# Leaving out three junk matmuls in the run-up of a fused recurrence and gated-MLP kernel

## The chip, the cores and the metric

The kernel runs on one core of a Trainium2 chip. The metric is the device time of one execution in microseconds; before the change it is 146.53 us, the median of three runs (146.23 to 146.56). The profiled execution has a span of 144.7 us from the first to the last instruction, and all times below count from the start of that span.

The engines are named as in the profile: PE is TensorE (PEld its weight loads), DVE VectorE, ACT ScalarE, POOL GpSimd, and SP the engine that issues the DMA transfers.

## The reference

Two stages follow each other. The first is a gated linear recurrence over 768 positions for 4 batches of 8 heads of 48 columns; the second an MLP with a spatial gate on the result. Cut to what matters:

```python
# q, k, v, alpha: (4, 8, 768, 48) fp32
for t in range(S):
    state = alpha[:, :, t, :, None] * state + einsum('bhd,bhe->bhde', k[:, :, t], v[:, :, t])
    y[:, :, t] = einsum('bhd,bhde->bhe', q[:, :, t], state)
x = y.transpose(0, 2, 1, 3).reshape(4, 768, 384)

h = maximum(x @ w_in, 0)                     # w_in: 384 x 1024
u, v = h[..., :512], h[..., 512:]
v_n = (v - mean(v)) / sqrt(var(v) + 1e-6)
v_s = einsum('ts,bsd->btd', w_spatial, v_n) + b_spatial[None, :, None]
out = (u * v_s) @ w_out                      # (4, 768, 384) fp32
```

## The kernel before

The recurrence is computed in chunks of 128 positions, six for each batch, 24 in all. Within a chunk the products over time are matrix products: PE sums log(alpha) with a triangular matrix (`cum`), ACT takes exponentials of the sums with both signs (`binv`, and the bank itself), k is multiplied with the one and q with the other (`kt`, `qt`, on DVE or POOL), PE transposes both (L481), ACT or DVE copies the transposes out of PSUM (`kqT`), PE forms the scores (L553), DVE masks them (`ptm`, L564), and PE multiplies the masked scores with v (L580) and q with the state so far (L593). The state goes from chunk to chunk through PE (L523), DVE (L330 and L332), POOL (L337) and a bf16 copy by POOL (`sbd`, L199). The first eight chunks are taken two at a time, in pairs, whose halves are the even and odd positions; pair 0 and pair 1 are the run-up that the change touches. The MLP of a batch follows its chunks and is interleaved with the chunks of later batches.

All PSUM tiles come from one ring of eight banks: the function `bank` hands them out in turn, so that each PE operation that needs a bank takes the one whose last reader is eight turns back. A matmul into a bank waits for the engine that still reads it.

The order on all engines is written out by hand in the string `PLAN`. Each word is a letter for the engine (P for PE, D for DVE, A for ACT, G for POOL, S for SP, Q for the arrival of a transfer) and the number of an operation. `replay` emits the words one after the other; each engine works through its own words in this order, and a scheduler changes nothing in it.

A word of PE may carry numbers after colons. `replay` puts them into the list `fill`, and `bank`, when the operation asks for its first bank, first writes a junk matmul of so many columns into that bank (L187): the constant tile `junk`, 128 x 128 in fp32, against itself, with a result that nobody reads, because the operation proper overwrites the bank. Junk matmuls give PE something to do while it would be idle. The program has 17 of them, in the first 20 us; each shows as two records in the trace. A junk matmul needs the bank free, as the operation proper does, but not that operation's data.

The words whose junk changes, with the operations that they stand for:

- `P111:64`, the transposes of q for pair 1, even positions (`tr` in the function `pair`, L481). Their data is `qt` from DVE (L460). The bank was last read by that same operation.
- `P109:512`, the transposes of k for pair 1, even positions (L481). Their data is `kt` from DVE (L453). The bank was last read by ACT, which copied earlier q transposes out of it (`kqT`, L197).
- `P182:128`, the first cumulative sums of pair 2 (`cum`, L431). Their data is log(alpha) from ACT (`la`, L422). The bank was last read by DVE, which masked scores of pair 0 (L564).

Behind them on PE stand, in this order: after `P111` the scores of pair 0 (`P71`), its state products (`P63:160`, L515 and L523), the other scores (`P74`); then `P109`; after it the other transposes of k (`P119:256`, data from POOL, L453), the spatial bias spread over the partitions (`P241`, L823), the scores of pair 1 (`P131:256` and `P134`, L553); then `P182`, the other sums (`P172`), the state products of pair 1 (`P123:160`), and the masked scores of both pairs with v (`P77` and `P137`, L580).

Of the kernel before, what the change touches and what calls it, by code (L numbers as in the profile page):

```python
# [56 lines left out]
PLAN = """  # L57
S34 S94 G0 S36 S38 Q35 D1 Q95 S98 A42 Q37 S40 P53:512:512:192 P43:64 A102 G32 Q33 A44 Q39 S96 P103:160 A54 P113 D46
A55 G56 A45 D2 Q99 A104 S163 P49:448 G3 A105 P59:64 D57 A50 D47 A114 Q41 S100 A115 P51:512:64 D117 A52 P243:96 P61
D107 P121 A62 Q97 S167 D60 P111:64 D244 P71 A48 G58 D72 P63:160 Q164 S4 P74 D65 A64 A112 D106 G66 A122 Q101 S165  # L60
G116 D68 P109:512 D73 G69 D75 P119:256 P241 Q168 G70 S9 A120 D110 D76 A171 P131:256 P134 D133 A242 G108 P182:128 Q5
S169 D132 P172 G118 A173 D135 G67 P123:160 A183 D136 A174 P77 A124 D125 A184 P137 D176 Q166 A78 S301 G126 P81 D186
P79 G127 A82 P138 D128 A80 P83 A139 P142 Q10 P190 A84 D6 G8 P140 P180 A143 D7 A141 D175 G185 S14 P88 P144 D181 G129
A89 P188 D191 Q170 P178 S305 G130 A145 D189 P85 A179 D90 G12 P200 A86 P197 Q302 P146 S303 D199 A187 G177 P157 D198
A11 G13 P192 D202 Q15 A158 S18 D201 P153 A193 A147 D194 P203 D87 G195 P155 A309 G196 D148 P204 Q306 S307 P151 A205
P208 D154 P320 A209 P206 D156 P310 A91 G16 Q304 P210 D17 P149 A207 D159 A211 S22 P229 A311 P223 A321 D93 Q19 S361
P212 D152 A312 G313 A322 D314 P225 A160 D324 P215 A150 G323 D92 A213 P231 D230 Q308 P316 A224 S363 P221 D162 A216
D161 G20 P318 D232 A226 P326 P227 A222 D217 G21 Q23 S402 P328 A317 P233 A329 D319 P235 D214 A234 P338 A228 G315 D327
P253 A218 D339 Q362 G325 S365 P249 A236 D219 P330 D220 Q364 D340 S367 P341 P245 D332 Q403 A369 D343 P254 S406 A331
A24 P250 G333 D255 Q366 P370 A25 S404 D251 P246 D342 P237 A371 G252 Q368 P239 S26 A410 D335 P257 D247 A238 G256 P411  # L70
Q407 D240 P258 S438 A372 A374 G373 P261 A412 D259 Q405 P262 A413 S408 A376 D375 G336 A415 P344 D263 G334 Q27 P377
S471 A345 P265 D378 G414 D379 P348 P269 D416 A349 P346 G248 P350 A347 P266 A351 G260 P418 D267 Q439 P384 S440 A419
P270 D386 G337 A420 P355 Q409 D385 S442 P380 P352 D271 A356 G28 Q472 D381 A29 P387 S473 G272 A446 P425 A388 Q441
# [1046 lines left out]
```

## Time and profile before

| | busy us of 144.7 | of this, 13.9 to 17.3 us |
|---|---|---|
| PE | 136.3 | 2.48 of 3.40 |
| DVE | 121.9 | 2.61 |
| ACT | 108.6 | 1.14 |
| POOL | 86.4 | 2.39 |

The second column is the page's account of the whole span; the third is the busy time in the stretch around the largest of the three junk matmuls, from the view of windows. A share of the whole span is an average over stages: the run-up, in which each engine waits for the one before it, and the long stretch from about 40 us on, in which PE is busy nearly all the time (19.48 of 20 us from 60 to 80, 20.00 of 20 from 80 to 100).

All 34 records of junk (two for each junk matmul) are busy for 12.1 us in all and lie between 1.1 and 20.4 us. Before 34 records of junk the page counts 2.1 us of idle time, 1.1 of it the wait for the constant tile at the start.

The DMA engines read 23.60 MB and write 4.72 MB. Their mean busy share is 0.9 or more in nearly all slices up to about 108 us.

### The profile page before, as it was taken

To read this page: it belongs to the slowest core of one execution; us is meant where nothing else is said; L and a number is where in the kernel's file an instruction comes from. 1 tells how busy PE (TensorE), PEld (TensorE's weight loads), DVE (VectorE), ACT (ScalarE), POOL (GpSimd) and SP (SyncE) were. 2 spreads that over 40 slices of the span, in tenths; PEclk is the share of its full clock that TensorE was granted. 3 is DMA by queue.
4 is the path that set the end of the run, shared out by engine and by line. 5 is a ranking of instruction groups with operands and counts; after the bars stand their busy time and mean duration, and the time that the engine had idled before them with its cause. 6 is when DMAs were issued, how large, how long until landed. Compare 5 with 4: busy or idle time off the path is not lost.

```text
span 144.7 us, 4779 instructions
## 1 busy us (share of the span) xinstructions
PE 136.3 (94%) x1849; PEld 88.0 (61%) x1849; DVE 121.9 (84%) x276; ACT 108.6 (75%) x271; POOL 86.4 (60%) x148
## 2 busy tenths in 40 slices
PE   7899798999899999989999999999999999999990
PEld 3467486666666666556666676666666766566560
DVE  6567879899998779998988998999799989996940
ACT  3594479879998689989989799999947867870051
POOL 5851839755616988966429997942379893002900
PEclk9999999999999999999999999999999999999999
DMA  4999999999999999999979989899996008086035
GB/s 114 268 261 261 289 335 306 304 299 328 213 205 272 174 201 177 193 183 175 205 132 194 182 169 201 158 197 158 206 207 139 0 7 326 5 304 245 0 137 190
DMA packets 88999, 28.62 MB, mean 198 GB/s; under 512 B 83728, under 2 KB 87440, under 8 KB 88976
## 3 DMA queue, kind: packets, MB, share of 16 engines
q1 hardware_dynamic: 88944, 28.32, 89.1%
q8 instruction: 14, 0.23, 0.7%
q14 instruction: 9, 0.07, 0.2%
q0 software_dynamic: 32, 0.00, 0.0%
HBM read 23.60 MB, written 4.72 MB: 196 GB/s over the span
## 4 chain that ended last, share of the span: by engine, by line
PE 70%; DVE 11%; ACT 7%; POOL 3%; DMA 3%; issue 2%; SPq 0%; POOLq 0%; DVEq 0%; ACTq 0%
PE bank L798 47%; DMA ac<-in_alpha_dram 3%; PE bank L724 3%; PE bank L689 3%; PE bank L187 2%; DVE ptm L735 2%; PE bank L366 2%; DVE vn L891 2%; PE bank L752 2%; ACT binvp L439 2%; DVE ptm L564 2%; PE bank L636 2%; ACT bank L448 2%; PE bank L710 1%; PE bank L746 1%
## 5 line engine op out<-in xcount | busy, mean ns | idle before, releaser
L798 PE MATMUL bank<-w_spT,vn 128*128 128x384 bf16 x192 | 36.5, 326 | 0.0
L953 POOL TENSOR_TENSOR gT<-vsb,uT 128x384 bf16<-128x384 f32 x29 | 26.3, 924 | 15.5 <-DVE vsb L940 14.9
L798 PEld LDWEIGHTS <-vn 128*128 128x128 bf16 x192 | 17.0, 97 | 10.5 <-issue 0.4
L735 DVE TENSOR_TENSOR ptm<-bank,mask 128x512 bf16<-128x512 f32 x32 | 21.0, 685 | 2.6 <-PE bank L724 2.4
L337 POOL TENSOR_TENSOR state<-state,bc 128x192 f32<-128x192 f32 x20 | 10.4, 521 | 19.8 <-DVE state L330 11.0
L798 PE MATMUL bank<-xT,w_in 128*128 128x384 bf16 x96 | 19.9, 326 | 0.0
L798 PE MATMUL bank<-w_in,xT 128*128 128x512 bf16 x72 | 19.3, 379 | 0.0
L940 DVE TENSOR_TENSOR vsb<-bank,bsp_bc 128x384 f32<-128x384 f32 x31 | 16.3, 552 | 3.2 <-PE bank L798 2.9
L660 POOL TENSOR_TENSOR kt<-kc,binv 128x384 bf16<-128x384 f32 x16 | 14.7, 924 | 6.8 <-ACT binv L648 5.4
L798 PE MATMUL bank<-w_out_sb,gT 128*128 128x384 bf16 (+1 forms) x100 | 18.2, 319 | 0.0
L197 ACT COPY kqT<-bank 128x512 bf16<-128x512 bf16 x21 | 11.8, 594 | 4.7 <-PE bank L481 2.4
L197 ACT CAST x_sb<-bank 128x384 bf16<-128x384 f32 x24 | 11.4, 481 | 4.1 <-PE bank L752 2.3
L187 PE MATMUL bank<-junk 128*128 128x512 f32 (+7 forms) x34 | 12.1, 455 | 2.1 <-DVE junk L233 1.1
L859 DVE BATCH_NORM_STATS2 stats<-v_sb 128x6 f32<-128x512 bf16 x20 | 13.6, 682 | 0.2 <-ACT v_sb L203 0.2
L199 POOL CAST sbd<-state 64x192 bf16<-64x192 f32 x36 | 12.5, 348 | 1.9
L203 ACT ACTIVATE v_sb<-bank 128x512 bf16<-128x512 f32 x20 | 11.9, 601 | 1.3 <-PE bank L798 1.1
L798 PEld LDWEIGHTS <-gT 128*128 128x128 bf16 x100 | 9.2, 98 | 5.3
L891 DVE TENSOR_SCALAR vn<-v_sb,mvs,rstd 128x512 bf16<-128x512 bf16 x24 | 10.7, 475 | 1.9 <-ACT rstd L884 1.9
L197 ACT COPY xT<-bank 128x384 bf16<-128x384 bf16 x24 | 11.2, 483 | 1.3 <-PE bank L366 1.0
L564 DVE TENSOR_TENSOR ptm<-bank,mask 128x512 bf16<-128x512 f32 x16 | 10.4, 684 | 1.5 <-PE bank L553 1.5
L199 DVE COPY kqT<-bank 128x512 bf16<-128x512 bf16 x27 | 10.6, 412 | 0.7 <-PE bank L481 0.6
L798 PEld LDWEIGHTS <-w_in 128*128 128x128 bf16 x96 | 8.2, 97 | 4.9
(127 smaller groups left out, 288.0 us busy)
## 6 DMA issues: line engine op xcount, KB each, us to landing
ac<-in_alpha_dram SPq DMA_DIRECT2D x16, 192.0 KB, 4.8
kc<-in_k_dram SPq DMA_DIRECT2D x16, 192.0 KB, 4.8
qc<-in_q_dram SPq DMA_DIRECT2D x16, 192.0 KB, 4.2
vc<-in_v_dram SPq DMA_DIRECT2D x16, 192.0 KB, 4.5
raw_w<-in_moe_w_spatial_dram SPq DMA_DIRECT2D x3, 768.0 KB, 5.6
out_dram<-raw_w SPq DMA_DIRECT2D x11, 192.0 KB, 2.3
out_dram<-o_sb SPq DMA_DIRECT2D x9, 192.0 KB, 2.1
ac<-in_alpha_dram SPq DMA_DIRECT2D x4, 384.0 KB, 5.6
```

Of the source, the lines that this page charges most:

```text
L187: nc.tensor.matmul(out=flat[:, 0:cols].rearrange("p (a b) -> p a b", a=4), lhsT=junk, rhs=junk[:, None, 0:n].to_broadcast([128, 4, n]), st ...
L197: nc.scalar.copy(out=out, in_=in_)
L199: ENG[eng].tensor_copy(out=out, in_=in_)
L203: nc.scalar.activation(out=out, in_=in_, func=AF.Relu)
L564: nc.vector.tensor_tensor(out=st[f"ptm{par}"][:, s], in0=st[f"pt{s}{par}"], in1=mask2[:, par], op=ALU.mult)
L660: ENG[eng].tensor_mul(out=k_blocks(kt3)[:, :, :, 0:D], in0=quad(st["kc"]), in1=st["binv"])
L735: nc.vector.tensor_tensor(out=st["ptm"][:, s], in0=st[f"pt{s}"], in1=mask4, op=ALU.mult)
L798: return lambda ps: nc.tensor.matmul(out=out(ps), lhsT=lhsT(), rhs=rhs(), start=start, stop=stop)
L859: nc.vector.bn_stats(out=stats, in_=d["v_sb"][:, tt, :])
L891: nc.vector.tensor_scalar(out=d["vn"][:, t, :], in0=d["v_sb"][:, t, :], scalar1=d["mvs"][:, t, 0:1], scalar2=d["rstd"][:, t:t + 1], op0=AL ...
L940: nc.vector.tensor_tensor(out=hold["vs"], in0=ps[:, 0:TH], in1=bsp_bc[:, th, :], op=ALU.add)
L953: ENG[eng].tensor_tensor(out=bt[b]["gT"][:, dsl, cols], in0=hold["vs"], in1=bt[b]["uT"][:, dsl, cols], op=ALU.mult)
```

## The change

Three junk matmuls are left out: 64 columns ahead of `P111`, 512 ahead of `P109`, and 128 ahead of `P182`. These are junk matmuls whose bank comes free late, so that the junk itself waits for it. What waited for the bank in the junk's stead is then the operation proper. The other 14 junk matmuls stay, and on each engine the order of all other instructions is the same. The diff, without the lines that only differ in where they are broken:

```diff
-D107 P121 A62 Q97 S167 D60 P111:64 D244 P71 A48 G58 D72 P63:160 Q164 S4 P74 D65 A64 A112 D106 G66 A122 Q101 S165
+D107 P121 A62 Q97 S167 D60 P111 D244 P71 A48 G58 D72 P63:160 Q164 S4 P74 D65 A64 A112 D106 G66 A122 Q101 S165
-G116 D68 P109:512 D73 G69 D75 P119:256 P241 Q168 G70 S9 A120 D110 D76 A171 P131:256 P134 D133 A242 G108 P182:128 Q5
+G116 D68 P109 D73 G69 D75 P119:256 P241 Q168 G70 S9 A120 D110 D76 A171 P131:256 P134 D133 A242 G108 P182 Q5
```

More of the change, by code (lines that the diff above doesn't have):

```diff
@@ L59 @@
 A55 G56 A45 D2 Q99 A104 S163 P49:448 G3 A105 P59:64 D57 A50 D47 A114 Q41 S100 A115 P51:512:64 D117 A52 P243:96 P61
-D107 P121 A62 Q97 S167 D60 P111:64 D244 P71 A48 G58 D72 P63:160 Q164 S4 P74 D65 A64 A112 D106 G66 A122 Q101 S165
-G116 D68 P109:512 D73 G69 D75 P119:256 P241 Q168 G70 S9 A120 D110 D76 A171 P131:256 P134 D133 A242 G108 P182:128 Q5
-S169 D132 P172 G118 A173 D135 G67 P123:160 A183 D136 A174 P77 A124 D125 A184 P137 D176 Q166 A78 S301 G126 P81 D186
-P79 G127 A82 P138 D128 A80 P83 A139 P142 Q10 P190 A84 D6 G8 P140 P180 A143 D7 A141 D175 G185 S14 P88 P144 D181 G129
@@ L64 @@
[L64 to L68, printed above, removed]
@@ L69 @@
-P253 A218 D339 Q362 G325 S365 P249 A236 D219 P330 D220 Q364 D340 S367 P341 P245 D332 Q403 A369 D343 P254 S406 A331
-A24 P250 G333 D255 Q366 P370 A25 S404 D251 P246 D342 P237 A371 G252 Q368 P239 S26 A410 D335 P257 D247 A238 G256 P411
+D107 P121 A62 Q97 S167 D60 P111 D244 P71 A48 G58 D72 P63:160 Q164 S4 P74 D65 A64 A112 D106 G66 A122 Q101 S165 G116
+D68 P109 D73 G69 D75 P119:256 P241 Q168 G70 S9 A120 D110 D76 A171 P131:256 P134 D133 A242 G108 P182 Q5 S169 D132
+P172 G118 A173 D135 G67 P123:160 A183 D136 A174 P77 A124 D125 A184 P137 D176 Q166 A78 S301 G126 P81 D186 P79 G127
@@ new lines @@
+A82 P138 D128 A80 P83 A139 P142 Q10 P190 A84 D6 G8 P140 P180 A143 D7 A141 D175 G185 S14 P88 P144 D181 G129 A89 P188
+D191 Q170 P178 S305 G130 A145 D189 P85 A179 D90 G12 P200 A86 P197 Q302 P146 S303 D199 A187 G177 P157 D198 A11 G13
+P192 D202 Q15 A158 S18 D201 P153 A193 A147 D194 P203 D87 G195 P155 A309 G196 D148 P204 Q306 S307 P151 A205 P208 D154
+P320 A209 P206 D156 P310 A91 G16 Q304 P210 D17 P149 A207 D159 A211 S22 P229 A311 P223 A321 D93 Q19 S361 P212 D152
+A312 G313 A322 D314 P225 A160 D324 P215 A150 G323 D92 A213 P231 D230 Q308 P316 A224 S363 P221 D162 A216 D161 G20
@@ L71 @@
+P318 D232 A226 P326 P227 A222 D217 G21 Q23 S402 P328 A317 P233 A329 D319 P235 D214 A234 P338 A228 G315 D327 P253
+A218 D339 Q362 G325 S365 P249 A236 D219 P330 D220 Q364 D340 S367 P341 P245 D332 Q403 A369 D343 P254 S406 A331 A24
+P250 G333 D255 Q366 P370 A25 S404 D251 P246 D342 P237 A371 G252 Q368 P239 S26 A410 D335 P257 D247 A238 G256 P411
 Q407 D240 P258 S438 A372 A374 G373 P261 A412 D259 Q405 P262 A413 S408 A376 D375 G336 A415 P344 D263 G334 Q27 P377
```

## The prediction

> **What bounds the kernel now.** I read the page from the top down. The first part gives each engine's busy time over the 144.7 us span, the fourth the chain of work that ended last; its shares are summed over the whole span.
>
> ```profile
> PE 136.3 (94%) x1849; PEld 88.0 (61%) x1849; DVE 121.9 (84%) x276; ACT 108.6 (75%) x271; POOL 86.4 (60%) x148
> ...
> PE 70%; DVE 11%; ACT 7%; POOL 3%; DMA 3%; issue 2%; SPq 0%; POOLq 0%; DVEq 0%; ACTq 0%
> ```
>
> PE is the bound on average, but not everywhere. The windows view shows PE busy 20.00 of 20 us from 80 to 100, and only 1.08 of 2 us from 14 to 16. The edited matmuls all run between 12 and 20 us, in the run-up, so the average says nothing about them. The chain in order of time, for that stretch (start, length, engine, what):
>
> ```profile
> 14.50 0.97 ACT kqT L197 x2
> 15.48 0.04 issue
> 15.52 1.13 PE bank L187 x2
> 16.64 0.22 PE bank L481 x4
> 16.87 0.49 PE bank L187 x2
> ...
> 17.84 0.63 PE bank L187 x2
> 18.47 0.38 PE bank L553 x16
> 18.85 0.02 issue
> 18.87 2.28 DVE ptm L564 x4
> ```
>
> L187 is the junk. The chain runs *through* it: ACT's evacuation frees a bank, a junk matmul of 512 columns starts, and the k transposes (L481), the scores (L553) and DVE's masking (L564) follow. Now PE's own timeline (start, length, group, idle before and its releaser), where the starts matter more than the lengths, since neighbouring matmuls overlap:
>
> ```profile
> 12.13 0.41 PE L187 MATMUL bank<-junk 128*128 128x64 f32 x2 [0.16 <-DVE qt L460]
> 12.37 0.39 PE L481 MATMUL bank<-ident,qt 128*128 128x128 bf16 x4
> ...
> 15.52 1.13 PE L187 MATMUL bank<-junk 128*128 128x512 f32 x2 [0.92 <-ACT kqT L197]
> 16.48 0.39 PE L481 MATMUL bank<-ident,kt 128*128 128x128 bf16 x4
> 16.70 0.65 PE L187 MATMUL bank<-junk 128*128 128x256 f32 x2
> 17.19 0.39 PE L481 MATMUL bank<-ident,kt 128*128 128x128 bf16 x4
> 17.51 0.33 PE L823 MATMUL bank<-b_sp_sb,ones_row 1*128 1x384 bf16 x1
> 17.77 0.70 PE L187 MATMUL bank<-junk 128*128 128x256 f32 x2
> 18.40 0.64 PE L553 MATMUL bank<-kqT 48*64 48x128 bf16 x32
> ```
>
> The reader is to see that the first two junk groups are preceded by idle time: they don't fill the wait, they sit behind it (each writes a bank that a reader still holds), and then hold up real work. Their price is from start to start: 12.37 - 12.13 = 0.24 us for 64 columns, 16.48 - 15.52 = 0.96 us for 512. The third, 128 columns, starts at 18.97, and the cumulative sums (L431) behind it at 19.30: 0.33 us.
>
> [...] 0.96 us for 512 fp32 columns, against 0.22 us from start to start in the bf16 512-column stream (L798, six from 27.13 to 28.43). [...] Hence the junk's wait isn't removed with it; it passes to the transpose or sum that writes the same bank next. The trace shows such a wait (0.92 us on ACT's evacuation). [...] the first junk group, 1216 columns, took 4.01 us (3.3 ns a column), where the later one took 0.96 us for 512 (1.9 ns). No fall-back during the work is seen: PEclk stays at 1.00 in every window from 2 to 120 us. [...]
>
> **The change, part by part.** Nothing is added or reordered.
>
> *64 columns, ahead of a q transpose.* That transpose reads DVE's product qt, which releases the junk too: its start moves from 12.37 to about 12.13. The scores behind it (12.69) need an ACT evacuation that ran from 11.65 to 12.24, so they can follow to 12.45. Then come state products (13.68 to 13.44) and, on their end, ACT's bc, two ACT evacuations (14.40) and DVE's state (14.29), kt and masks. DVE's load for kt landed at 13.59, before its new 14.32. All of these move by 0.24; the evacuation that frees the bank ends at 15.23, not 15.47.
>
> *512 columns, ahead of a k transpose.* The transpose gets the wait and starts at 15.52 - 0.24 = 15.28 instead of 16.48. Its data, DVE's kt (14.56 + 0.55 = 15.11, now 14.87), is ready. Next the 256-column junk (16.70 - 16.48 = 0.22 later) at 15.50[...]. The second k transpose could start at 16.03, but needs POOL's kt, 15.44 + 0.92 = 16.36 before, 16.12 now; with 0.05 for the signal, 16.17. Here **a new wait takes back about 0.14**. Then the bias row at 16.17 + 0.32 = 16.49, junk at 16.49 + 0.26 = 16.75, scores at 16.75 + 0.63 = 17.38, against 18.40: a move of 1.02. The scores' other need, DVE's copy of kqT (16.98 + 0.42 = 17.40, now 17.16), is met. DVE's masks follow at 18.87 - 1.02 = 17.85; DVE itself is free at 18.00 - 0.24 = 17.76. So the masks move by 1.02, and DVE alone would not allow more than 1.11. I take 1.0.
>
> *128 columns, ahead of the sums.* The sums now need ACT's la, which ran from 18.10 to 18.95 behind an evacuation that waited 2.15 us for PE; both move by about 1.0, so la ends at 17.95 and the sums, otherwise free at 17.97, start at 18.0 instead of 19.30, a move of 1.3. But the last products of that group (L580, 20.91, 64 of them, the last starting at 21.79) wait for DVE's four masks, and so do DVE's state (21.27) and POOL's (21.79) behind them. I cost this part at **nothing**: the masks' 2.48 us hide it.
>
> *From 20 us on.* State (DVE 21.27, POOL 21.79), state copies (POOL 22.37), the next kt (POOL 24.07) and its transposes (25.34) hang one on another, so the 1.0 us passes on if no load stops it. The completion records of the loads, set against first use, give the slack: k of the third pair 22.73 against 23.56 (0.83), v of it 26.19 against 27.14 (0.95), the second third of w_spatial 34.83 against 35.75 (0.92); all loads from 39 us on have 1.8 us or more. So three of them bind by up to 0.2. None is on the chain: the k load stops DVE's kt (its new end, 22.78 + 0.95 = 23.73, is before the transposes' new 24.36) and DVE idles 0.60 us at 25.78 anyway; the v casts are needed at 28.71; POOL's w_spatial casts end at 37.4 for transposes at 38.4. Cost: nothing. In 40 to 141 us PE runs full in its fixed order and the whole schedule slides.
>
> Sum: -0.24 - 0.96 + 0.14, rounded with the 0.04 of slack in signals, is about -1.0; 146.53 - 1.0 = **145.5 us**. Bounds: 0.74 if the 64-column part gains nothing (0.96 - 0.22, POOL's kt not moving), 1.11 if DVE alone limits.
>
> **The rivals.**
>
> *A load takes over.* DMA engines are in use at 0.9 or more in nearly every slice up to 108 us, so loads won't land earlier. For it: the 0.83 us slack. Against it: what such a load stops has slack of its own. If it binds in full, 0.8 of gain, 145.7; if the prefetch ring takes back half later, 146.0.
>
> *Nothing arrives at the end.* Early time saved is lost where PE, in its fixed order, meets other engines, as at 39.79, where it has waited 0.6 us for DVE. Against it: DVE there works without a break from 34.73, on inputs that would themselves be earlier. 146.5.
>
> *The clock falls back, slower.* The junk between 13.9 and 17.3 us is most of PE's array work there: 2.48 us busy of 3.40, from which about 1 us goes. [...] Against it: from 22.0 to 25.4 PE does little more than short transposes and products, with no junk, and later matmuls keep their full-rate spacing; the longest gap stays near 0.9 us.
>
> **How the numbers follow.** Full pass 0.62 (145.5, give or take 0.25 for the run and the signals); capped by a load or in part 0.17 (145.7 to 146.1); nothing 0.09 (146.5); clock 0.09 (147.2); a little more than reckoned 0.03 (145.2). The range, 145.15 to 146.35, leaves out the clock, most of "nothing" and a tail. Faster by over 0.3% means below 146.09: 0.62 + 0.13 + 0.03 = 0.78. Within 0.3%: 0.11. Slower: 0.09 and 0.02 of noise, 0.11.
>
> **What would show it.** In the new timeline the k transposes should start near 15.3 with ACT's kqT as releaser, the next ones near 16.2 with POOL's kt as releaser, the scores near 17.4, DVE's four masks near 17.9, POOL's kt near 23.1, and the last matmul to end near 140.3 instead of 141.3. I am wrong if the masks move by less than 0.7, if POOL or DVE idle on a DMA between 22 and 38 us, or if bf16 matmuls of 384 columns come 0.32 us apart after 15 us instead of 0.16.

## The result, and the profile after

The changed kernel takes **145.66 us** (median of 4 runs, 145.63 to 145.91) against 146.47 (146.23 to 146.56): ratio 0.9951, 95% interval 0.9934 to 0.9968. The profiled span fell from 144.7 to 143.9 us. In three of the experiments the ratio leaves out executions that took about 2 us or more longer than the fastest (4 of 14 in padded, 4 of 21 in after5, 13 of 22 in shifted_back, and 7 of these 13 at a full mean clock, for which no cause was found), so that their medians lie above what the ratio says.

The page of the changed kernel, engines and shares of the chain:

```profile
PE 135.1 (94%) x1831; PEld 87.6 (61%) x1843; DVE 121.6 (85%) x276; ACT 108.7 (76%) x271; POOL 86.4 (60%) x148
...
PE 67%; DVE 10%; ACT 7%; POOL 6%; DMA 3%; issue 3%; SPq 0%; POOLq 0%; ACTq 0%; DVEq 0%
```

PEld, the weight loads, count 6 fewer (three fp32 junk matmuls, two records each); PE counts 18 fewer because 12 records of matmuls are missing from this trace. Two shares have grown. POOL has 6% where it had 3%: in the run-up the chain no longer passes through the junk ahead of the k transposes but from DVE's state (13.96) through POOL's state, kt and copies and ACT's exponentials to DVE's next state (20.16), which DVE reaches from its masks at about the same moment. "issue" has 3% where it had 2%, which turns out to matter.

PE's timeline in the run-up (start, length, group, idle before and its releaser):

```profile
15.17 0.38 PE L481 MATMUL bank<-ident,kt 128*128 128x128 bf16 x4 [0.91 <-ACT kqT L197]
15.39 0.65 PE L187 MATMUL bank<-junk 128*128 128x256 f32 x2
16.06 0.40 PE L481 MATMUL bank<-ident,kt 128*128 128x128 bf16 x4
...
17.28 0.64 PE L553 MATMUL bank<-kqT 48*64 48x128 bf16 x32
17.88 0.65 PE L431 MATMUL bank<-la,le_pair 128*128 128x384 bf16 x3
```

The wait for ACT's evacuation hasn't gone: 0.91 us now stand ahead of the k transposes themselves, 0.92 stood ahead of the junk. But the transposes start at 15.17 instead of 16.48 and the scores at 17.28 instead of 18.40. DVE's four masks follow at 17.75 instead of 18.87. So at the end of the run-up the kernel is **1.12 us** ahead, more than its whole gain. Compared instruction by instruction, the lead is still 1.12 us at the transposes of k of the third pair, pair 2 (25.34 before, 24.22 now). It falls to 0.78 in the middle of that pair's scores and stays there to the last matmul. The chain of waits at that place (start, length, what):

```profile
24.22 0.62 PE bank L481 x8
...
24.89 0.59 PE bank L798 x2
25.49 0.46 PE bank L553 x23
25.94 0.13 issue
26.07 0.35 PE bank L553 x9
```

Thirty-two scores of one form, all with the same data, break into 23 and 9. The timeline of the weight loads shows the break more sharply, after the change:

```profile
25.41 0.36 PEld L553 LDWEIGHTS <-kqT 48*64 48x64 bf16 x23 [0.42 <-DVE kqT L199]
26.07 0.19 PEld L553 LDWEIGHTS <-kqT 48*64 48x64 bf16 x9 [0.29 <-issue]
```

and before it:

```profile
26.54 0.49 PEld L553 LDWEIGHTS <-kqT 48*64 48x64 bf16 x32 [0.42 <-DVE kqT L199]
```

"issue" means that no semaphore is waited for. PE has its data, its bank and nothing ahead of it, and yet does nothing for 0.29 us (0.34 from matmul to matmul). Where the 0.34 us went was the question for the experiments.

### The profile page after: what moved, and what is told of

It is laid out like the page before. It is cut to its first block, busy times and chain, and to the rows that moved or that the text cites. A ratio compares the mean times of both kernels' runs of the same rounds, so it can differ in the third digit from the quotient of the medians.

```text
span 143.9 us, 4754 instructions
## 1 busy us (share of the span) xinstructions
PE 135.1 (94%) x1831; PEld 87.6 (61%) x1843; DVE 121.6 (85%) x276; ACT 108.7 (76%) x271; POOL 86.4 (60%) x148
## 4 chain that ended last, share of the span: by engine, by line
PE 67%; DVE 10%; ACT 7%; POOL 6%; DMA 3%; issue 3%; SPq 0%; POOLq 0%; ACTq 0%; DVEq 0%
PE bank L798 47%; DMA ac<-in_alpha_dram 3%; PE bank L724 3%; PE bank L689 3%; ACT binvp L439 2%; DVE ptm L735 2%; PE bank L366 2%; DVE vn L891 2%; PE bank L752 2%; ACT bank L448 2%; PE bank L636 2%; POOL state L337 1%; PE bank L710 1%; POOL kt L453 1%; PE bank L746 1%
## 5 line engine op out<-in xcount | busy, mean ns | idle before, releaser
L735 DVE TENSOR_TENSOR ptm<-bank,mask 128x512 bf16<-128x512 f32 x32 | 21.0, 684 | 2.6 <-PE bank L724 2.4
L798 PE MATMUL bank<-w_in,xT 128*128 128x512 bf16 x60 | 17.3, 378 | 0.8 <-issue 0.2
L199 POOL CAST sbd<-state 64x192 bf16<-64x192 f32 x36 | 12.5, 348 | 1.9
L187 PE MATMUL bank<-junk 128*128 128x512 f32 (+6 forms) x28 | 10.6, 487 | 1.1 <-DVE junk L233 1.1
L199 DVE COPY kqT<-bank 128x512 bf16<-128x512 bf16 x27 | 10.6, 412 | 0.7 <-PE bank L481 0.6
L197 ACT COPY o_sb<-bank 128x384 f32<-128x384 f32 x9 | 4.3, 482 | 9.1 <-PE bank L798 9.1
```

Source lines behind the costliest of these rows:

```text
L187: nc.tensor.matmul(out=flat[:, 0:cols].rearrange("p (a b) -> p a b", a=4), lhsT=junk, rhs=junk[:, None, 0:n].to_broadcast([128, 4, n]), st ...
L197: nc.scalar.copy(out=out, in_=in_)
L199: ENG[eng].tensor_copy(out=out, in_=in_)
L735: nc.vector.tensor_tensor(out=st["ptm"][:, s], in0=st[f"pt{s}"], in1=mask4, op=ALU.mult)
L798: return lambda ps: nc.tensor.matmul(out=out(ps), lhsT=lhsT(), rhs=rhs(), start=start, stop=stop)
```

## The experiments

Each edit below is told against the kernel before, as words of `PLAN`. The three series ran beside their own runs of the kernel before: 146.53 us median (after_again, only512, padded, late_out), 146.42 (after5, shifted, only64, only128) and 146.54 (shifted_again, shifted_back).

**Is the stop an accident of one execution?** The changed kernel again.

> The changed kernel once more, for its trace. In the first trace all engines ran 1.12 us earlier than before from the masks at 17.75 on, and from 26.1 us on only 0.78 us, because PE stopped for 0.34 us in the middle of the 32 score products of pair 2 (L553, 25.73 to 26.07) without a wait that the trace names. Theory A (the stop belongs to the program as it now runs, such as PE's instructions arriving late): the stop is there again, within 0.05 us of its place and length, and the span is 143.9. Theory B (a chance of that one execution, or of its recording): it is gone or elsewhere, and the span is 143.5 to 143.6.

145.4 us in one run. The stop is there again, at the same instruction, but the rest is not as theory A had it: the stop is shorter, and the span is 143.6 us, the figure of theory B. Two more things differ in this trace. The load of k for the third pair is complete at 23.02 us (22.74 in the first trace), and POOL's kt, which reads it too and stands on the chain, waits for it:

```profile
23.04 0.56 DVE L453 TENSOR_TENSOR kt<-kc,binvp 128x384 bf16<-128x384 f32 x1 [0.56 <-DMA kc<-in_k_dram]
23.16 1.21 POOL L453 TENSOR_TENSOR kt<-kc,binvp 128x384 bf16<-128x384 f32 x1 [0.20 <-DMA kc<-in_k_dram]
```

And near 37 us a lead of 0.3 us comes back. The changed kernel was timed once more, with more executions:

> The changed kernel itself, timed in five rounds. It has the place of the instruction boundary seen so far: PE's stop stands at the 352nd weight load of PE's stream (counted from 0: 351) in all five kernels that leave junk out, which have between 4 and 28 instructions fewer than before ahead of it, and it ends 1.4 to 1.6 us after the second 16 KB transfer of instructions to PE lands. Theory A (PE waits for its own instructions): stop at weight load 351 again, ending 1.5 us after that transfer's end; time 145.4 to 145.7. Theory B (a chance of the execution): no stop, or at another place.

Ratio 0.9939 (0.9916 to 0.9961). The stop is there a third time, at 26.05 us. In all three traces PE goes on with its weight load 351 (counted from 0). The gap from one weight load to the next is 0.40, 0.28 and 0.20 us, where about 0.015 us is the mean in the scores (0.49 us for 32). The lead over the kernel before, in us, of the same instructions:

| trace | masks | k transposes of pair 2 | behind weight load 351 | behind 37.3 us | end |
|---|---|---|---|---|---|
| the change | 1.12 | 1.12 | 0.78 | 0.78 | 0.79 |
| after_again | 1.18 | 0.92 | 0.69 | 1.01 | 1.01 |
| after5 | 1.25 | 0.95 | 0.80 | 1.12 | 0.96 |

So all three lose at weight load 351, and the last two lose 0.26 and 0.30 us more ahead of it: in after5, too, POOL's kt starts (23.12) only when the k load is complete (22.99).

**The large junk alone.**

```diff
-P109:512
+P109
```

> Only the 512-column junk is left out; the 64 and the 128 columns stay. By the prediction's steps the masks of pair 1 (L564) move from 18.87 to about 18.1, by 0.72 to 0.78 (0.96 less the wait for POOL's kt), and the cumulative sums of pair 2 by about as much. The end: if PE's stop near 25.7 ends at a fixed time near 26.1, because something arrives then, PE comes there at about 26.1 and there is no stop: the whole 0.75 arrives, 145.7, the same as with all three out. If the stop has a fixed length of 0.34 us at that place in the program, 0.4 arrives, 146.05. If the 64 columns were what helped, no change, 146.47.

Median 146.21 us, ratio 0.996 (0.9938 to 0.9982). This is later than either of the two forecasts with a gain. The masks are 0.85 us earlier (0.07 of it from ahead of the changed place), and the kernel loses most of it soon after. Its weight loads:

```profile
25.68 0.31 PEld L553 LDWEIGHTS <-kqT 48*64 48x64 bf16 x19 [0.42 <-DVE kqT L199]
26.57 0.25 PEld L553 LDWEIGHTS <-kqT 48*64 48x64 bf16 x13 [0.58 <-issue]
```

The scores arrive later than in the changed kernel (25.68, not 25.41), the stop is longer (0.69 us) and ends later, and it stands after 19 scores, not 23. So it is neither a fixed moment nor a fixed length. The 19 and 23 are the clue: this kernel has two junk matmuls more ahead of the scores, four weight loads, and four scores fewer before the stop. It is **weight load 351** again. What is fixed is a place in PE's stream of instructions.

**The small ones alone.**

```diff
-P111:64
+P111
```

> Only the 64 columns are left out. By the prediction's steps the q transpose starts 0.24 us earlier; the first trace of the change showed 0.34, for the junk had waited about 0.1 us longer for its bank's two signals than the transpose does. So 0.34 at the first masks (13.21 to 12.87) and still 0.34 at the masks of pair 1 (18.87 to 18.53). At PE's weight load 351 the 256 instructions before it take 5.9 us as before: stop between 0 and 0.3 us. The end is then 146.1 to 146.4.

146.53 us in one run, more than was expected. The q transposes start at 11.97 instead of 12.37, and the lead of 0.39 us holds to 26.8; then the stop, 0.54 us at weight load 351, takes all of it and 0.1 us more.

```diff
-P182:128
+P182
```

> Only the 128 columns are left out. The cumulative sums of pair 2 start 0.3 us earlier (19.30 to 19.0), and so do ACT's exponentials, but DVE's four masks (18.87) and all that hangs on them do not move: the end is the same, 146.4 to 146.6, less or more by what the stop at weight load 351 does, which PE now reaches after entering the block 0.3 us earlier: 0 to 0.3 us.

146.43 us in one run. The sums start earlier by 0.30 against the work around them, and the masks don't move against it. (All work from 11.5 us on, ahead of the changed place as behind it, is 0.25 us later here than in the kernel before, and the step near 37 us makes up for that; so the end, 0.01 us earlier, says less than the masks do.) No stop is seen.

**The same length of stream.** The three junk matmuls out, and three of 4 columns in, ahead of the first work:

```diff
-P53:512:512:192
+P53:512:512:192:4:4:4
-P111:64
+P111
-P109:512
+P109
-P182:128
+P182
```

> The three junk matmuls are left out as in the change, and three junk matmuls of 4 columns are added to those ahead of the first cumulative sums, where PE waits for the first load (idle from 5.06 to 5.52 before). PE's program has the length of that of before, so that each later instruction stands at the place in the instruction stream that it had before; the time of PE's work from 6 us on is that of the changed kernel. If PE's stop comes from where the boundaries of the instruction stream fall, it vanishes or moves: the end is 1.1 us earlier than before, 145.35. If it comes from the time at which something arrives, or from the place in the program, it stays: 145.7 as with the change. If the three tiny ones delay the first sums, up to 0.1 us is lost again.

Ratio 0.9954 (0.9914 to 0.9994). The profiled execution had a granted clock of 0.50 from 15.12 to 21.95 us, so its times can't be set beside the others. Its stop is at weight load 351 too, 0.16 us. The interval is too wide to say more, and which of the two forecasts holds stays open.

**All junk after 12 us out** (`P63:160`, `P119:256`, `P131:256` and `P123:160` besides the three):

```diff
-P63:160
+P63
-P119:256
+P119
-P131:256
+P131
-P123:160
+P123
```

> All junk behind 12 us is left out: besides the three also 160 columns ahead of the state products of both pairs, 256 ahead of the other k transposes and 256 ahead of the first scores of pair 1. By the prediction's steps: state products 0.3 us earlier again, so the second k transposes at about 15.8 (POOL's kt), the scores at 16.8 (DVE's copy of kqT is then last), the masks at about 17.3 to 17.4, that is 0.35 us earlier than with the change; then the load of k of pair 2 (landing 22.74) holds POOL's kt at 22.8, and 0.2 of it is lost: 1.3 us earlier than before at 24 us. If PE's stop near 25.7 ends at a fixed time, all of that goes and the end is as with the change, 145.7. If the stop has a fixed length, 1.3 - 0.34: 145.5. If there is no stop, 145.2. If the array's clock falls back without the junk, products of 384 columns come 0.32 us apart for some us after 15 us, and the end is 146.5 to 147.5.

Median 146.01 us, ratio 0.9939 (0.9919 to 0.996). Two things happen. The first is the clock. In the windows view (sum, busy time and instructions of PE, PEld, DVE, ACT and POOL, PEclk, DMA share, GB/s):

```profile
16.00:20.00 4.00, 3.99 (x77) 2.54 (x77) 3.85 (x7) 2.30 (x5) 2.53 (x7) 0.50 1.12 325
20.00:22.00 2.00, 2.00 (x85) 1.94 (x80) 1.63 (x6) 1.53 (x5) 0.97 (x3) 0.50 1.12 334
```

and in PE's timeline of the same kernel:

```profile
17.85 1.14 PE L431 MATMUL bank<-la,le_pair 128*128 128x384 bf16 x3
```

The same three sums took 0.65 us in the changed kernel, whose PEclk is 1.00 from 16 to 20 us; from the first of them to the L431 behind the third it is 0.94 us here (17.85 to 18.79), 0.31 a sum, and 0.48 there (17.88 to 18.36), 0.16 a sum. Of the 1.55 us by which the scores of pair 1 lead, 0.83 are left at 25 us; the clock of 0.50 is in this loss, but the k load, complete at 22.77, would have taken part of it at any clock. The clock fell, as the last forecast had it, and yet the end is not at 146.5 or later. Every one of its 22 runs has a mean clock of 0.988 or less, and no other kernel here lost the clock in all its runs, so the small junk behind the change does seem to have a use. The second thing is the stop, 0.55 us at weight load 351 (after 31 scores: eight weight loads fewer ahead of them than in the changed kernel). In the profiled execution, 146.19 us, it leaves 0.2 us of lead to the end.

**Moving the place.** If the stop stands at a place in the stream, fewer instructions ahead of the scores put that place behind them. `shifted` is the change with six more small junk matmuls out, each four instructions (two weight loads, two matmuls):

```diff
-P43:64
+P43
-P103:160
+P103
-P59:64
+P59
-P51:512:64
+P51:512
-P243:96
+P243
-P123:160
+P123
```

> The three junk matmuls of the change are left out and six small ones more (64, 160, 64, 64, 96 columns before 12 us, 160 ahead of the state products of pair 1, where PE waits for DVE's masks afterwards anyway): 24 instructions fewer ahead of the scores of pair 2 than in the changed kernel. Weight load 351 is then the first of the 512-column products behind the scores (L798), and the 256 instructions before it take PE about 6.8 to 7.0 us instead of 6.2, since these products are long. Theory A (instructions arrive about 6.5 us after PE enters the block before): no stop, or under 0.1 us, in the scores; what is gained by 25 us, 1.1 to 1.4 us, reaches the end: 145.1 to 145.4. Theory B (the stop belongs to the scores, whatever the instruction stream): a stop of 0.3 us stays there, 145.6. If the array's clock falls back for a while, products of 384 columns come 0.32 us apart in the trace, and the time is 146 or more.

Median 145.19 us (145.16 to 145.41, 8 runs), ratio 0.9903 (0.9868 to 0.9939): faster than the kernel before. Its median is below that of the changed kernel as well, but the interval overlaps that of after5, so that this is not shown. The weight loads of the scores are whole:

```profile
25.52 0.48 PEld L553 LDWEIGHTS <-kqT 48*64 48x64 bf16 x32 [0.42 <-DVE kqT L199]
```

and the lead of 1.02 us at the masks is 1.01 at the end (near 37 us it is 1.36 for a while, and falls back by 39.8). Weight load 351 is now one of the products behind the scores, needed at 26.54 us.

But `shifted` has less junk work as well. So a last pair on one chip: `shifted` again, and `shifted_back`, which is `shifted` in all but the first junk group, where PE waits for data; there it has six matmuls more, tiny ones:

```diff
-P53:512:512:192
+P53:512:512:4:4:4:4:4:4:4
```

> The same kernel as `shifted` (the change, and six more junk matmuls of 64 to 160 columns out), measured again beside `shifted_back`. Both theories: 145.2 us, a ratio of about 0.990, no gap within the scores of the third pair, and the masks' gain of about 1.0 us held to the end.

> `shifted`, but the junk group of 512, 512 and 192 columns ahead of the first work is written as 512, 512 and seven of 4 columns: six matmuls more, 24 instructions of TensorE more, all before 8 us, where TensorE waits for the first data, so that the stream of instructions ahead of the third pair's scores is as long again as in the changed kernel while the junk from 12 us on is `shifted`'s. Theory of the refill (TensorE stops where a block of 256 instructions ends whose successor hasn't come): the gap is back, 0.2 to 0.4 us, at TensorE's weight load number 351, in the middle of the scores of the third pair, and the gain falls from 1.0 to 0.6-0.8 us: 145.4 to 145.6 us, slower than `shifted_again` by 0.2 to 0.4. Rival (the lesser junk from 43:64 to 123:160 itself makes `shifted` faster, by its own TensorE time): no gap in the scores, same time as `shifted_again` within 0.1 us. A gap of 0.2 us or more that is given back later would speak for neither.

`shifted_back`, weight loads:

```profile
25.62 0.36 PEld L553 LDWEIGHTS <-kqT 48*64 48x64 bf16 x23 [0.42 <-DVE kqT L199]
26.21 0.19 PEld L553 LDWEIGHTS <-kqT 48*64 48x64 bf16 x9 [0.22 <-issue]
```

The stop is back, after 23 scores as in the changed kernel, 0.33 us from weight load to weight load, and the lead falls there from 0.93 to 0.65 us. Six matmuls of 4 columns that end long before did this; the junk's work from 12 us on is the same. The times point the same way without proving it: ratio 0.9922 (0.9897 to 0.9947) against 0.991 (0.9873 to 0.9948), intervals that overlap. And `shifted_again` missed its expectation in an instructive way. Its profiled execution took 146.1 us, and its weight loads show this:

```profile
26.06 0.33 PEld L798 LDWEIGHTS <-xT 128*128 128x128 bf16 x3
26.93 0.33 PEld L798 LDWEIGHTS <-xT 128*128 128x128 bf16 x3 [0.54 <-issue]
```

The stop, now behind the scores, at weight load 351 once more. So `shifted` doesn't remove it; it gives PE more time before that place is reached, and in this execution it wasn't enough. The same trace has a second stop, 128 weight loads earlier, at weight load 223, where no other trace has one:

```profile
19.92 0.81 PEld L580 LDWEIGHTS <-ptm 64*128 64x128 bf16 x47 [0.44 <-issue]
```

It costs nothing, since these products would have waited for DVE's masks anyway. (This execution lost 0.3 us twice more, near 88 and 97 us, with PE waiting for DVE's qt; why, is open.)

**What stands at that place.** The page lists a queue that carries no data of the kernel:

```profile
q8 instruction: 14, 0.23, 0.8%
```

Fourteen transfers of 16,384 bytes, spread over the whole span. The trace gives the time of each; the second matters here. It lands while PE works from weight load 223 to 351, that is, through 128 weight loads and 128 matmuls, 256 instructions (all times in us):

| kernel | weight load 223 | transfer starts | ends | weight load 351 | gap ahead of it | 351 after the end |
|---|---|---|---|---|---|---|
| before | 20.86 | 24.25 | 25.47 | 26.78 | 0.04 | 1.31 |
| the change | 19.52 | 23.32 | 24.54 | 26.07 | 0.40 | 1.53 |
| after_again | 19.46 | 23.42 | 24.63 | 26.16 | 0.28 | 1.53 |
| after5 | 19.39 | 23.30 | 24.52 | 26.05 | 0.20 | 1.53 |
| only512 | 20.04 | 23.81 | 25.06 | 26.57 | 0.69 | 1.51 |
| only64 | 20.50 | 24.16 | 25.38 | 26.89 | 0.54 | 1.51 |
| late_out | 20.29 | 23.96 | 25.19 | 26.76 | 0.55 | 1.57 |
| shifted_back | 19.45 | 23.47 | 24.72 | 26.21 | 0.33 | 1.49 |
| shifted_again | 19.92 | 24.17 | 25.41 | 26.93 | 0.64 | 1.52 |
| padded | 22.19 | 25.59 | 26.80 | 28.16 | 0.16 | 1.36 |
| shifted | 19.50 | 23.53 | 24.78 | 26.54 | 0.22 | 1.76 |
| only128 | 20.84 | 24.29 | 25.51 | 26.99 | 0.00 | 1.48 |

Wherever PE stopped, it went on 1.36 to 1.57 us after the transfer's end, whichever operation stood there. The second stop of `shifted_again` fits: in its trace the transfer before this one ran from 17.16 to 18.39 us, later than in any other, and PE went on 1.53 us after its end. In the kernel before, PE came to the place 1.31 us after the end and didn't stop, and in only128 1.48 us after it: just in time. A lead ahead of the place is then lost as far as the transfer doesn't move with it: with the 64 columns out PE begins the 256 instructions 0.36 us earlier, and the transfer starts only 0.09 us earlier. In `shifted`, 0.22 us is the usual distance of two 512-column products; it came 1.76 us after the end, and didn't stop either. All this fits a PE that stops when it is through with 256 instructions and the transfer of the next has not come in time. That is the author's reading of these times and of `shifted_back`; the trace names no wait there. The 256 rest on two figures: in `shifted_again` the two stops stand 128 weight loads and 128 matmuls apart, and the kernel before has 1849 of each for 14 transfers, 264 instructions to a transfer. At this one place of the changed kernel the stop takes back 0.34 us of 1.12.

## Why the prediction was right, and where it was off

In the run-up the mechanism was as predicted, and the time came out close: 145.5 said, 145.66 measured. But the path from 20 us on was not as predicted, and two misses of opposite sign are in the time, 0.12 us more gained in the run-up and 0.34 us lost behind it. That they partly cancel is luck.

*64 columns.* Right in kind, too small: 0.36 us at the q transposes (12.37 to 12.01), not 0.24. The price from start to start left out that the transpose in the junk's place starts 0.12 us earlier than the junk did (12.13), on the same product of DVE: a semaphore instruction of PE (L187, 12.02, 0.05 us) stands ahead of the junk, and it is gone with it.

*512 columns.* Right: ACT's evacuation is the releaser, and the transposes start at 15.17 (15.28 said, the difference from the step before). POOL's kt took back 0.18 us (1.31 of lead at the first k transposes, 1.13 at the second), 0.14 said. The 0.53 us between 15.50 and 16.03, for the 256-column junk, was the author's estimate; the profile before has 0.49 from the start of this junk to the transposes behind it (16.70 to 17.19). Scores 17.28 (17.38), masks 17.75 (17.85): moved by 1.12, where DVE's bound was put at 1.11 and 1.0 was taken.

*128 columns.* Right. The sums start 1.42 us earlier, but the second half of the products behind them (L580) moves by 1.12 and waits 0.22 us for DVE's masks; in only128 the masks don't move against the work around them.

*From 20 us on.* This is the step that failed, in the words "Cost: nothing" and "the whole schedule slides". In the first trace the loads went as it said. DVE's kt waits for the k load, after the change:

```profile
22.76 0.63 DVE L453 TENSOR_TENSOR kt<-kc,binvp 128x384 bf16<-128x384 f32 x1 [0.24 <-DMA kc<-in_k_dram]
```

It ends at 23.39, and the transposes it feeds start at 24.22, released by POOL's kt; nothing is lost. The v casts wait 0.2 and 0.3 us for their load, hidden too. The transfer that PE's stop followed has no consumer in any list of loads: it is one of the queue `instruction`, and PE went on 1.53 us after its end. The term was 0 in the sum and measures 0.34: 1.12 - 0.34 = 0.78, against 144.7 - 143.9 = 0.8 in the spans.

The term for the loads itself was too small as well. It set the k load against DVE's kt and found slack behind that; but POOL's kt reads the same load, stands on the chain, and came to start at 22.95. The load is complete between 22.69 and 23.02 us in all twelve traces, whether PE is early or late. In the first trace it came in time (22.74); in after_again and after5 it cost 0.26 and 0.30 us. That "none is on the chain" held in the first trace is luck, too.

*The rivals.* "A load takes over" came nearest: it named a transfer as what takes back part, and its 145.7 is the measured time. In the first trace the transfer was not the load that it meant; in the two other traces of the changed kernel the k load did take part of the gain. "Nothing arrives" fell at 39.79, where PE's wait for DVE is 0.57 us, as before, so that DVE moved along. "The clock falls back" did not come true: PEclk is 1.00 from 12 to 52 us. The loss of 1.7 us in its 147.2 was an estimate of the author's that rests on no trace. late_out shows that it wasn't idle talk. With four more junk matmuls out, the clock stood at 0.50 from 15.57 to 22.40 us, 6.83 us; yet it cost at most 0.7 us (the lead of 1.55 at 0.83).

## What to carry to other kernels

Filler ahead of real work isn't free when it waits for the same buffer as that work: look for filler with idle time ahead of it (0.92 us ahead of the 512 columns here), and price it from its start to the start of the work behind it (0.96 us). When a lead shrinks at one instruction and nothing is waited for, count instructions rather than microseconds: here the stop stood at weight load 351 in nine of twelve traces, and leaving out or adding idle instructions ahead of it moved it to other work. Whether that pays has to be timed (here medians of 145.2 and 145.3 us against 145.7 and 145.8, with intervals that overlap). Where a stretch of very short instructions runs while loads keep the DMA engines full (here 256 in 5.9 to 7.0 us, and 335 GB/s in the changed kernel), look for the transfers of the queue `instruction`, and for what PE does behind their ends. And set a load against all its readers: the one with slack says nothing about the others.

## What the hardware showed that I had not expected

- **PE can stop with its data and its bank at hand.** From weight load 223 to 351, 256 instructions, it took 6.0 to 7.0 us wherever it stopped, and it went on 1.36 to 1.57 us after the end of a 16,384-byte transfer of the queue `instruction`. In the kernel before it was through in 5.9 us without a stop, so that the length alone doesn't decide. It is the only such place in the changed kernel: the first transfer ends 2.8 us ahead of weight load 223, and the others 4.5 us or more ahead of 479, 607 and so on, by 128.
- **The transfer starts late where loads are dense.** In the changed kernel it starts 3.80 us after weight load 223 at 19.5 us, while all transfers move 335 GB/s, 3.16 and 2.43 us after weight loads 351 and 479 (347 and 307 GB/s), and 0.3 to 1.7 us in eight of the ten stretches of 128 weight loads from 44 us on, where they move 191 GB/s up to 108 us. (In the two others it starts 0.15 and 2.3 us ahead of the weight load counted, so that the count of 128 weight loads may not be exact there.) That it waits behind the loads is argued from this and was not tried by taking loads away. Nor is it known what the further 1.5 us after its end are.
- **The clock can fall with PE at work.** In late_out and in padded it was at 0.50 for 6.83 us in both; from 16 to 20 us PE was busy for 3.99 and 4.00 us of 4 at this clock. Ahead of it, from 12 to 15 us, PE was busy for 2.02 us in late_out and for 2.25 in padded, at a clock of 1.00. How much work is enough to hold the clock was not measured.
- **A late load can help.** Near 37 us PE waits 0.16 us for a copy by DVE (L199) in the kernel before. In five traces (after_again, after5, shifted, shifted_again, only128) the copy comes 0.3 us earlier against the work ahead of it, and by 39.8 none, part or all of that is given back (none in after_again, all in shifted). In these five, DVE's vn ahead of the copy takes 0.41 to 0.53 us, in the seven others 1.04 or 1.05; the change and after5:

```profile
34.90 1.04 DVE L891 TENSOR_SCALAR vn<-v_sb,mvs,rstd 128x512 bf16<-128x512 bf16 x1
34.87 0.41 DVE L891 TENSOR_SCALAR vn<-v_sb,mvs,rstd 128x512 bf16<-128x512 bf16 x1
35.31 1.66 POOL L199 CAST w_row<-raw_w 128x768 bf16<-128x768 f32 x2 [0.21 <-DMA raw_w<-in_moe_w_spatial_dram]
```

  The third line is POOL's in after5. In the five traces POOL's cast begins 0.09 to 0.23 us after POOL's kt, in after5 and shifted because its load comes late, and vn is done by then or nearly so; in the seven it begins at once, and vn runs beside it. That the cast slows vn is argued from this and was not tried.
